# Cluster order of the last batch in a routed-attention and PReLU-MLP kernel: ranks found over three halves, one VectorE piece a slot, counts' product apart from the sums' product

## The chip, the cores and the metric

The kernel runs on one core of a Trainium2 chip. The metric is the device time of one execution in microseconds, median of three runs; less is better. Engines are named as in the profile: PE is TensorE, PEld its weight loads, DVE is VectorE, ACT is ScalarE, POOL is GpSimd, SP is the queue that issues most transfers.

## The reference

Inputs are q, k and v of 4 batches x 8 heads x 768 tokens x 64 features, 16 centroids a head, and the weights of a two-layer MLP of 512 -> 2048 -> 512 with a slope for each hidden unit.

```python
q_assign = np.argmax(np.einsum('bhsd,hcd->bhsc', q_n, c_n), axis=-1)
k_assign = np.argmax(np.einsum('bhsd,hcd->bhsc', k_n, c_n), axis=-1)
mask = q_assign[:, :, :, None] == k_assign[:, :, None, :]
scores = np.where(mask, scale * np.matmul(q, k.transpose(0, 1, 3, 2)), -1e9)
attn = softmax(scores)                      # over the keys of the same cluster
out = np.matmul(attn, v)                    # (B,H,S,D) -> x of (B*S, H*D)
h = x @ w_in
return (np.maximum(h, 0) + alpha * np.minimum(h, 0)) @ w_out
```

A query attends only to keys whose nearest centroid is its own. The MLP takes all heads of a token together.

## The kernel before

Heads are taken in pairs, four pairs a batch, sixteen in all (`n` = 0 to 15). A pair of batches 0 to 2 is worked off in two halves of 384 queries; the four pairs of the last batch (`n` = 12 to 15) are worked off whole. A half, or a whole pair of the last batch, is three *steps*, and from step 24 on its work is dealt out over 12 *slots* (two in the first step, five in each of the others). What a slot holds is written out by hand: `tick()` first runs the pieces that `later(slots, piece)` has put off to this slot, then one entry of `todo` (the masks and sums of the attention), then one entry of `sorting` (scatter work), then `feed` gives a share of MLP pieces of the *batch before*, so that PE always has dense work: a `hidden(f)` piece (four matmuls, L973, its copy out of PSUM on ACT, L979, and its slope on DVE, L965) or a `final` piece (four matmuls, L991). Each engine runs its own list in the order in which these Python calls emit instructions; the tile framework adds the waits.

The `todo` list of a half (L1173 to L1190) is: three masks, the five additions of the six exponentials (`add_up`, L770), `turn` (L789) and `rows_sums` (L795, writes `part`), two empty entries, and, in the half's last slot, `total` (L805): a small matmul that adds up the softmax denominators from `part`. Its result is written into `misc()`, a PSUM tile `mps` of a pool with **one** buffer (L89). Whatever matmul writes `mps` next waits until the reader of the last one is done. In the next half's beginning `invert` takes reciprocals of the total (L815), and `normalise` (L949) makes `xT`, the MLP's input.

The last batch is not masked over all keys. Its tokens are first put in the order of their clusters, so that a chunk of 128 queries need only see the neighbouring chunks of keys. That order is found ahead of time, in the middle of batches 1 and 2, at the steps `ORDERS = [30, 36, 54, 60]` (each the first step of a half), one for each pair:

- `load(n)` brings q and k, one step ahead;
- `order_features` (L535, two DVE transposes of 128x768) in steps t, t at slots 2 and 3;
- `order_sims` (L544), four matmuls with the centroids into `mps`, at t+1;
- `order_counts` (L549) one slot later: `argmax` (L376 to L393: transpose, maximum, compare, times rank, maximum), `only_first` (L396), a transpose to `mine` (L555) and a running count (`tensor_tensor_scan`, L557). These are eight DVE instructions in one go;
- `order_begins` (L564) at t+2, slot 2: two small matmuls of the counts, into `mps`;
- `order_ranks` (L572 to L592) one slot later: `begin` and `begins` are read from `mps` (L572, L573), then four more DVE instructions give each token its row, `off` (L581), and fill the `sorting` queue; `order_clusters` (L594) one slot later, three DVE instructions.

So everything from the transposes to the ranks falls in one half. After it the `sorting` entries load rows into two `stage` tiles (SP, L614) and scatter them into `scratch` in HBM (POOL, L625). Four steps before pair n begins (`u - 4`), `order_load` reads the sorted rows back (L636 to L654); `prep_clusters` (L425) makes the key clusters at `u - 3`, through `mps` and an ACT copy `every` (L429). After the attention of a pair in the last batch, `normalise_near` (L888) puts its result back in token order: `to_rows` (L911) turns it through `mps` in two parts, later by 4 and 6 slots, `put_back` (L919) scatters twelve pieces from slot 8 on, and `fetch_back` (L931) reads them at slot 14.

Of the kernel before, what the change touches and what calls it, by code (L numbers as in the profile page):

```python
# [23 lines left out]
def kernel(  # L24
# [70 lines left out]
    def later(slots, piece):  # L95
        due.setdefault(now[0] + slots, []).append(piece)
# [277 lines left out]
                             start=True, stop=True)  # L374
        later(1, lambda: prep_argmax(n, ps))

    def argmax(ps):
        simT = asg.tile([P, HS], FP32, name="simT")
        nc.vector.transpose(out=simT, in_=ps[:, 0:HS])
        sim = simT.rearrange("p (t c) -> p t c", c=NC)  # L380


        mx = asg.tile([P, 2 * NX], FP32, name="mx")
        nc.vector.tensor_reduce(out=mx, in_=sim, axis=AX.X, op=ALU.max)
        top = asg.tile([P, 2 * NX, NC], BF16, name="top")
        nc.vector.tensor_tensor(
            out=top, in0=sim, in1=mx[:, :, None].broadcast_to((P, 2 * NX, NC)),
            op=ALU.is_ge)
        nc.vector.tensor_tensor(
            out=top, in0=top, in1=rank[:, None, :].broadcast_to((P, 2 * NX, NC)),  # L390
            op=ALU.mult)
        first = asg.tile([P, 2 * NX], BF16, name="first")
        nc.vector.tensor_reduce(out=first, in_=top, axis=AX.X, op=ALU.max)  # L393
        return top, first

    def only_first(top, first):  # L396
        nc.vector.tensor_tensor(
            out=top, in0=top, in1=first[:, :, None].broadcast_to((P, 2 * NX, NC)),
            op=ALU.is_equal)

    def prep_argmax(n, ps):
        top, first = argmax(ps)
        firsts[n] = first
        if n >= NCH:
            return
        only_first(top, first)
        member = memp.tile([P, 2, HS], BF16, name="member")
        nc.vector.transpose(out=member[:, 0, :], in_=top.rearrange("p t c -> p (t c)"))

        def of_heads():  # L410
            for h in (1, 0):
                nc.scalar.activation(
                    out=member[HP:P, h, :], in_=member[HP:P, 0, :], func=AF.Identity,
                    scale=pick[HP:P, h:h + 1], bias=pick[HP:P, h + 2:h + 3])

        members[n] = member
        later(12 if n == 0 else 7, of_heads)
# [130 lines left out]

    def order_counts(n, ps):  # L549

        ordp = sorts["ordp"]
        top, first = argmax(ps)
        only_first(top, first)
        member = ordp.tile([P, HS], BF16, name="mine")
        nc.vector.transpose(out=member, in_=top.rearrange("p t c -> p (t c)"))  # L555
        count = asg.tile([P, HS], FP32, name="simT")
        nc.vector.tensor_tensor_scan(count, member, member, 0.0, ALU.add, ALU.max)  # L557
        us[n] = member, count

    def order_begins(n):  # L560
        member, count = us[n]
# [6 lines left out]
    def order_ranks(n, ps):  # L568
        member, count = us.pop(n)
        ordp, order = sorts["ordp"], sorts["order"]  # L570
        begin = ordp.tile([P, 2], FP32, name="begin")
        nc.vector.tensor_tensor(out=begin, in0=ps[:, 0:2], in1=sorts["shift"], op=ALU.add)  # L572
        nc.vector.tensor_copy(out=sorts["begins"][:, n - NO:n - NO + 1], in_=ps[:, 0:1])  # L573
        nc.vector.scalar_tensor_tensor(out=count, in0=count, scalar=begin[:, 1:2],
                                       in1=member, op0=ALU.add, op1=ALU.mult)
        by_token = ordp.tile([P, NX, 2, NC], FP32, name="by_token")
        nc.vector.transpose(out=by_token.rearrange("p x h c -> p (x h c)"), in_=count)
        rank = ordp.tile([P, NX, 2], FP32, name="rank")
        nc.vector.tensor_reduce(out=rank, in_=by_token, axis=AX.X, op=ALU.add)
        off = order.tile([P, NX, 2], I32, name="off")  # L580
        nc.vector.tensor_scalar(out=off, in0=rank, scalar1=0.0, scalar2=float(2 * S - 1),  # L581
                                op0=ALU.max, op1=ALU.min)
        ranks[n] = off
        whole = tc.dram_tile([2 * 2 * S, P], FP32, name=f"scratch{n}")
        scratch[n] = whole, dram_disjoint_views(whole, 2 * NX)
        for i in range(2 * PARTS + STAGES):
            if i >= STAGES:
                for x in range(NX // PARTS):
                    sorting.append(lambda i=i - STAGES, x=x: order_scatter(n, i, x))
            if i < 2 * PARTS:  # L590
                sorting.append(lambda i=i: order_stage(n, i))
        later(1, lambda: order_clusters(n, begin))  # L592

    def order_clusters(n, begin):  # L594
        ordp, order = sorts["ordp"], sorts["order"]
# [292 lines left out]
    def normalise_near(n):  # L888
        outT = inp.tile([P, 2, NJ, D], FP32, name="qk").rearrange("p h j d -> p (h j d)")
        for side in range(2):  # L890
            nc.vector.tensor_tensor(out=outT[:, side * HS:(side + 1) * HS],
                                    in0=pos.pop((n, side))[:, 0:HS],
                                    in1=rds.pop((n, side)), op=ALU.mult)
        whole = tc.dram_tile([2 * S, D], FP32, name=f"back{n}")
        to = dram_disjoint_views(whole, 2 * NJ)
        found = orders.pop(n)
        place = sorts["order"].tile([P, 2, NJ], I32, name="place")
        nc.vector.tensor_scalar(out=place, in0=found[:, :, :, 0], scalar1=0, scalar2=S - 1,
                                op0=ALU.max, op1=ALU.min)
        rows = sorts["byrow"].tile([P, NJ, P], FP32, name="rows")  # L900
        for i in range(2):
            later(4 + 2 * i, lambda i=i: to_rows(outT, rows, i))
        for i in range(2 * NJ):
            later(8 + i // 2, lambda i=i: put_back(to, place, rows, i))
        later(8 + NJ, lambda: fetch_back(n, whole))

    def to_rows(outT, rows, i):

        ps = misc()
        for j in range(HJ):  # L910
            nc.tensor.transpose(out=ps[:, j * P:(j + 1) * P],  # L911
                                in_=outT[:, (i * HJ + j) * P:(i * HJ + j + 1) * P],
                                identity=ident)
        later(1, lambda: nc.scalar.copy(  # L914
            rows[:, i * HJ:(i + 1) * HJ].rearrange("p j d -> p (j d)"), ps[:, 0:HS]))
# [109 lines left out]
    TOGETHER = 2 * UB  # L1025
    FREE = SLOTS * SB - 3

    ORDERS = [30, 36, 54, 60]
    prep_at, load_at = {}, {}
    for (n, half), u in start_of.items():  # L1030
        def at(step, slot, piece):
            prep_at.setdefault((step, slot), []).append(piece)
        if half is None:
            t = ORDERS[n - NO]
            load_at.setdefault(t - 1, []).append(lambda n=n: load(n))
            for i in range(2):
                at(t, FIRST + i, lambda n=n, i=i: order_features(n, i))
            at(t + 1, FIRST + 1, lambda n=n: order_sims(n))
            at(t + 2, FIRST, lambda n=n: order_begins(n))
            load_at.setdefault(u - 4, []).append(lambda n=n: order_load(n))  # L1040
            at(u - 3, FIRST, lambda n=n: prep_clusters(n))
            for i in range(2):
                at(u - 2, FIRST + i, lambda n=n, i=i: order_blocks(n, i))
                at(u - 1, FIRST + i, lambda n=n, i=i: order_queries(n, i))
            continue
        if half == 0:
            if n < NCH:
                if n > 1:
                    load_at.setdefault(max(u - 7, 0), []).append(lambda n=n: load(n))
                if n > 0:  # L1050
                    load_at.setdefault(max(u - 6, 0), []).append(lambda n=n: load_v(n))
            else:
                load_at.setdefault(u - 9, []).append(lambda n=n: load(n))
                load_at.setdefault(u - 7, []).append(lambda n=n: load_v(n))
            if n < NCH:
                for g in range(len(groups)):
                    at(u - 4, FIRST + g, lambda n=n, g=g: prep_features(n, g))
            else:
                for w in range(2):
                    at(u - 7, FIRST + w, lambda n=n, w=w: prep_blocks(n, w))  # L1060
            at(u - (3 if n < NCH else 5 if u - 6 < TOGETHER else 6), FIRST,
               lambda n=n: prep_sims(n))
            if n >= NCH:
                at(u - 4, FIRST, lambda n=n: prep_clusters(n))
        for h in range(2):
            at(u - 1, FIRST + h, lambda n=n, half=half, h=h: prep_queries(n, half, h))
# [363 lines left out]
```

## Time and profile before

| | |
|---|---|
| time, three runs | 1009.71, 1011.34, 1012.8 us; median 1011.34 us |
| profiled execution | span 1011.6 us, mean granted clock 0.989 |
| PE waits before `total` (L805) for `begins` (L573) | 12.0 us in 4 places, one at each order |
| scatters (L625) of the four pairs begin at | 298.57, 363.69, 549.42, 612.47 us |
| last batch's attention | about 699 to 807 us; from 840 us on only MLP is left |

The page gives for each engine its busy time. A busy engine isn't yet the bound: what counts is where PE stands still, for PE has the most work. The list of PE's waits names for each of its lines the instruction that ended the wait; the timeline of one engine shows what that instruction was queued behind. A matmul of fp32 operands shows as two records, so a `hidden` piece, four matmuls, is eight records. An ACT or DVE start in an answer may lie some hundredths of a microsecond before the end of its forerunner, since records overlap a little.

### The profile page before, as it was taken

To read this page: it belongs to the slowest core of one execution; us is meant where nothing else is said; L and a number is where in the kernel's file an instruction comes from. 1 tells how busy PE (TensorE), PEld (TensorE's weight loads), DVE (VectorE), ACT (ScalarE), POOL (GpSimd) and SP (SyncE) were. 2 spreads that over 40 slices of the span, in tenths; PEclk is the share of its full clock that TensorE was granted. 3 is DMA by queue.
4 is the path that set the end of the run, shared out by engine and by line. 5 is a ranking of instruction groups with operands and counts; after the bars stand their busy time and mean duration, and the time that the engine had idled before them with its cause. 6 is when DMAs were issued, how large, how long until landed. Compare 5 with 4: busy or idle time off the path is not lost.

```text
span 1011.6 us, 10921 instructions
## 1 busy us (share of the span) xinstructions
PE 974.3 (96%) x3955; PEld 484.7 (48%) x3955; DVE 655.0 (65%) x1209; ACT 259.6 (26%) x468; POOL 214.0 (21%) x249
## 2 busy tenths in 40 slices
PE   8889999999989999999999997999999999999997
PEld 5434444454444444545444444455554545455453
DVE  5887798598596785877859587678998723021010
ACT  5755443222221221312222122222132111110110
POOL 1423223000013534400002356300045440000000
PEclk9999999999999999999999998999999999999999
DMA  6533552050003422415000322600431120000000
GB/s 246 196 109 107 149 141 51 16 108 17 1 8 83 105 62 51 84 37 104 1 1 12 88 73 65 124 1 11 84 63 32 28 50 16 0 1 32 0 1 34
DMA packets 174286, 60.46 MB, mean 60 GB/s; under 512 B 161216, under 2 KB 164752, under 8 KB 174224
## 3 DMA queue, kind: packets, MB, share of 16 engines
q1 hardware_dynamic: 168768, 51.42, 21.5%
q0 software_dynamic: 4608, 7.87, 2.3%
q8 instruction: 33, 0.54, 0.2%
q10 hardware_dynamic: 848, 0.39, 0.2%
q14 instruction: 29, 0.24, 0.1%
HBM read 45.15 MB, written 14.16 MB: 59 GB/s over the span
## 4 chain that ended last, share of the span: by engine, by line
PE 84%; DVE 11%; ACT 2%; issue 2%; DMA 1%; ACTq 0%; DVEq 0%; POOL 0%; POOLq 0%
PE fps L991 32%; PE fps L973 27%; PE vps L849 8%; PE sps L719 7%; PE fps L719 3%; DVE acc L770 1%; DVE gT L965 1%; PE sps L728 1%; PE mps L371 1%; PE vps L885 1%; DVE acc L789 1%; DVE more L760 1%; DVE E L760 1%; DVE part L795 1%; ACT E L740 1%
## 5 line engine op out<-in xcount | busy, mean ns | idle before, releaser
L973 PE MATMUL fps<-xT,w_in_sb 128*128 128x384 f32 x1024 | 347.8, 494 | 0.8 <-issue 0.8
L991 PE MATMUL fps<-w_out_sb,gT 128*128 128x512 f32 x768 | 340.2, 598 | 3.4 <-issue 2.3
L973 PEld LDWEIGHTS fps<-xT,w_in_sb 128*128 128x128 f32 x1024 | 192.2, 192 | 140.9 <-issue 11.6
L991 PEld LDWEIGHTS fps<-w_out_sb,gT 128*128 128x128 f32 x768 | 144.2, 191 | 178.2 <-issue 168.1
L625 POOL DMA_INDIRECT scratch<-stage,off x96 | 104.8, 1092 | 291.8 <-DVE gT L965 125.8
L965 DVE SCALAR_TENSOR_TENSOR gT<-gT,alpha 128x384 f32<-128x384 f32 x128 | 80.3, 637 | 131.6 <-ACT gT L979 120.0
L979 ACT COPY gT<-fps 128x384 f32<-128x384 f32 x128 | 61.2, 478 | 364.6 <-PE fps L973 342.2
L719 PE MATMUL sps<-qkT 64*128 64x384 f32 (+1 forms) x512 | 96.5, 494 | 0.8 <-ACT E L740 0.8
L760 DVE SCALAR_TENSOR_TENSOR more<-aq,key,more 128x384 f32<-128x384 bf16 (+1 forms) x136 | 74.5, 603 | 24.2 <-ACT more L740 16.8
L740 ACT ACTIVATE E<-sps 128x768 f32<-128x768 f32 (+1 forms) x81 | 61.2, 801 | 78.0 <-PE sps L728 44.4
L919 POOL DMA_INDIRECT back<-rows,place x48 | 49.2, 1026 | 129.7 <-ACT rows L914 116.3
L999 DVE TENSOR_TENSOR y<-y,fps 128x512 f32<-128x512 f32 x30 | 20.6, 685 | 79.0 <-PE fps L991 79.0
L719 PEld LDWEIGHTS sps<-qkT 64*128 64x128 f32 x512 | 45.8, 186 | 45.1 <-issue 17.5
L849 PE MATMUL vps<-E,vt 128*64 128x384 f32 x356 | 66.6, 500 | 0.0
L760 DVE SCALAR_TENSOR_TENSOR E<-aq,key,E 128x384 f32<-128x384 bf16 (+1 forms) x104 | 57.1, 602 | 11.9 <-ACT E L740 6.7
L770 DVE TENSOR_TENSOR acc<-acc,E 128x768 f32<-128x768 f32 x47 | 44.9, 955 | 16.9 <-ACT E L740 15.4
L997 ACT COPY y<-fps 128x512 f32<-128x512 f32 x24 | 14.0, 585 | 135.1 <-PE fps L991 115.9
L740 ACT ACTIVATE more<-sps 128x768 f32<-128x768 f32 (+1 forms) x47 | 35.6, 796 | 40.2 <-PE sps L719 33.7
L849 PEld LDWEIGHTS vps<-E,vt 128*64 128x64 f32 x356 | 23.3, 138 | 32.6 <-issue 32.3
L849 PE MATMUL vps<-more,vt 128*64 128x384 f32 x220 | 38.8, 491 | 0.0
L269 POOL TENSOR_TENSOR w_in_sb<-w_in_sb,power 128x512 f32<-128x512 f32 x16 | 22.2, 1386 | 70.2 <-DVE w_in_sb L266 70.2
L719 PE MATMUL fps<-qkT 64*128 64x384 f32 x160 | 34.9, 508 | 0.0
(175 smaller groups left out, 731.4 us busy)
## 6 DMA issues: line engine op xcount, KB each, us to landing
raw<-in_moe_w_in_dram SPq DMA_DIRECT2D x16, 512.0 KB
raw<-in_moe_w_out_dram SPq DMA_DIRECT2D x16, 512.0 KB
out_dram<-y SPq DMA_DIRECT2D x24, 256.0 KB
vt<-in_v_dram SPq DMA_DIRECT2D x12, 384.0 KB
qk<-in_q_dram SPq DMA_DIRECT2D x48, 96.0 KB
qk<-in_k_dram SPq DMA_DIRECT2D x48, 96.0 KB
qk<-scratch SPq DMA_DIRECT2D x32, 96.0 KB
qk<-in_q_dram SPq DMA_DIRECT2D x4, 384.0 KB
```

What stands on the lines that cost most here:

```text
L269: nc.gpsimd.tensor_tensor(out=dst, in0=dst, in1=power[0].bitcast(FP32), op=ALU.mult)
L625: nc.gpsimd.indirect_dma_start(out=scratch[n][1][h * NX + xx], out_offset=bass.IndirectOffsetOnAxis(ap=ranks[n][:, xx, h:h + 1], axis=0), ...
L719: nc.tensor.matmul(out=bank(ps, h, m), lhsT=qkT[r:r + D, S + c * P:S + (c + 1) * P], rhs=qkT[r:r + D, tokens], start=True, stop=not early_ ...
L740: nc.scalar.activation(out=E[:, :, 0:m], in_=ps[:, :, 0:m], func=AF.Exp, scale=SCALE)
L760: nc.vector.scalar_tensor_tensor(out=e, in0=of, scalar=keys[n][:, NJ + c, h:h + 1], in1=e, op0=ALU.is_equal, op1=ALU.mult)
L770: nc.vector.tensor_tensor(out=acc, in0=acc if first is None else first[3], in1=E, op=ALU.add)
L849: nc.tensor.matmul(out=po[r:r + D, 0:HS], lhsT=vts[n][:, h, c, :], rhs=e[:, h, :], start=(c == 0), stop=(c == NJ - 1))
L919: nc.gpsimd.indirect_dma_start(out=to[i], out_offset=bass.IndirectOffsetOnAxis(ap=place[:, h, j:j + 1], axis=0), in_=rows[:, j, h * D:(h + ...
L965: nc.vector.scalar_tensor_tensor(out=gs[f], in0=gs[f], scalar=alpha[:, f:f + 1], in1=gs[f], op0=ALU.mult, op1=ALU.max)
L973: nc.tensor.matmul(out=ps[:, 0:HS], lhsT=w_in_sb[:, c, f * P:(f + 1) * P], rhs=xTs[b, half][:, c, :], start=(c == 0), stop=(c == NCH - 1))
L979: nc.scalar.copy(gs[f], ps[:, 0:HS])
L991: nc.tensor.matmul(out=ps[:, 0:DM], lhsT=gs[f][:, i * P:(i + 1) * P], rhs=w_out_sb[:, f, :], start=on and f == f0, stop=off and f == f0 + ...
```

## The change

The ordering of one pair is stretched over three halves, and its DVE instructions are dealt out one to a slot between the additions of the attention, in place of blocks of eight and six. Loads and transposes (`order_features`) come in the half before (t = `ORDERS` is three steps earlier, and they stand at t+2); the products with the centroids are at t+3, so in the same step of the same half as `ORDERS` before, one step earlier than the products were; the small matmuls of the counts (`order_begins`) move out of that half to the next one, t+7, away from the sums' product `total`. `order_ranks` is cut in two, the second part a slot later. `prep_clusters` moves from three to four steps before its pair. In the last batch `to_rows` comes 6 and 10 slots after `normalise_near` instead of 4 and 6, except for the very last pair, and each part's `put_back` follows two slots after it.

```diff
-    def argmax(ps):
+    def argmax(ps, exact):
...
+        pieces = [
+            lambda: nc.vector.transpose(out=simT, in_=ps[:, 0:HS]),
+            lambda: nc.vector.tensor_reduce(out=mx, in_=sim, axis=AX.X, op=ALU.max),
+            lambda: nc.vector.tensor_tensor(out=top, in0=sim, in1=wide(mx), op=ALU.is_ge),
...
     def prep_argmax(n, ps):
-        top, first = argmax(ps)
+        top, first, pieces = argmax(ps, exact=n < NCH)
+        for piece in pieces:
+            piece()
...
     def order_counts(n, ps):
-        top, first = argmax(ps)
-        only_first(top, first)
...
+        top, first, pieces = argmax(ps, exact=True)
...
+        for i, piece in enumerate(pieces):
+            later(i, piece) if i else piece()
...
+        later(1, lambda: order_rows(n, begin, count))
+
+    def order_rows(n, begin, count):
...
-        later(1, lambda: order_clusters(n, begin))
+        later(2, lambda: order_clusters(n, begin))
...
+        starts = (4, 6) if n == NP - 1 else (6, 10)
         for i in range(2):
-            later(4 + 2 * i, lambda i=i: to_rows(outT, rows, i))
-        for i in range(2 * NJ):
-            later(8 + i // 2, lambda i=i: put_back(to, place, rows, i))
-        later(8 + NJ, lambda: fetch_back(n, whole))
+            later(starts[i], lambda i=i: to_rows(outT, rows, i))
+            for x in range(NJ):
+                later(starts[i] + 2 + x // 2,
+                      lambda i=i, x=x: put_back(to, place, rows, i * NJ + x))
+        later(starts[1] + 2 + HJ, lambda: fetch_back(n, whole))
...
-    ORDERS = [30, 36, 54, 60]
+    ORDERS = [27, 33, 51, 57]
...
-            load_at.setdefault(t - 1, []).append(lambda n=n: load(n))
+            load_at.setdefault(t, []).append(lambda n=n: load(n))
             for i in range(2):
-                at(t, FIRST + i, lambda n=n, i=i: order_features(n, i))
-            at(t + 1, FIRST + 1, lambda n=n: order_sims(n))
-            at(t + 2, FIRST, lambda n=n: order_begins(n))
+                at(t + 2, 2 + 2 * i, lambda n=n, i=i: order_features(n, i))
+            at(t + 3, FIRST + 1, lambda n=n: order_sims(n))
+            at(t + 7, 2, lambda n=n: order_begins(n))
             load_at.setdefault(u - 4, []).append(lambda n=n: order_load(n))
-            at(u - 3, FIRST, lambda n=n: prep_clusters(n))
+            at(u - 4, FIRST, lambda n=n: prep_clusters(n))
```

More of the change, by code (lines that the diff above doesn't have):

```diff
@@ L375, in prep_sims, with wide @@
         later(1, lambda: prep_argmax(n, ps))
-    def argmax(ps):
+    def argmax(ps, exact):
         simT = asg.tile([P, HS], FP32, name="simT")
-        nc.vector.transpose(out=simT, in_=ps[:, 0:HS])
         sim = simT.rearrange("p (t c) -> p t c", c=NC)
         mx = asg.tile([P, 2 * NX], FP32, name="mx")
-        nc.vector.tensor_reduce(out=mx, in_=sim, axis=AX.X, op=ALU.max)
         top = asg.tile([P, 2 * NX, NC], BF16, name="top")
[L386 to L391, printed above, removed]
-        first = asg.tile([P, 2 * NX], BF16, name="first")
[L393 to L399, printed above, removed]
+        first = asg.tile([P, 2 * NX], BF16, name="first")
+        def wide(row):
+            return row[:, :, None].broadcast_to((P, 2 * NX, NC))
+        pieces = [
+            lambda: nc.vector.transpose(out=simT, in_=ps[:, 0:HS]),
+            lambda: nc.vector.tensor_reduce(out=mx, in_=sim, axis=AX.X, op=ALU.max),
+            lambda: nc.vector.tensor_tensor(out=top, in0=sim, in1=wide(mx), op=ALU.is_ge),
+            lambda: nc.vector.tensor_tensor(
+                out=top, in0=top, in1=rank[:, None, :].broadcast_to((P, 2 * NX, NC)),
+                op=ALU.mult),
+            lambda: nc.vector.tensor_reduce(out=first, in_=top, axis=AX.X, op=ALU.max)]
+        if exact:
+            pieces.append(lambda: nc.vector.tensor_tensor(
+                out=top, in0=top, in1=wide(first), op=ALU.is_equal))
+        return top, first, pieces
     def prep_argmax(n, ps):
-        top, first = argmax(ps)
+        top, first, pieces = argmax(ps, exact=n < NCH)
+        for piece in pieces:
+            piece()
         firsts[n] = first
@@ L549, in order_counts, with scan @@
     def order_counts(n, ps):
-        ordp = sorts["ordp"]
-        top, first = argmax(ps)
[L553 to L558, printed above, removed]
+        top, first, pieces = argmax(ps, exact=True)
+        member = sorts["ordp"].tile([P, HS], BF16, name="mine")
+        pieces.append(lambda: nc.vector.transpose(
+            out=member, in_=top.rearrange("p t c -> p (t c)")))
+        def scan():
+            count = asg.tile([P, HS], FP32, name="simT")
+            nc.vector.tensor_tensor_scan(count, member, member, 0.0, ALU.add, ALU.max)
+            us[n] = member, count
+        pieces.append(scan)
+        for i, piece in enumerate(pieces):
+            later(i, piece) if i else piece()
     def order_begins(n):
@@ L575, in order_ranks @@
                                        in1=member, op0=ALU.add, op1=ALU.mult)
+        later(1, lambda: order_rows(n, begin, count))
+    def order_rows(n, begin, count):
+        ordp, order = sorts["ordp"], sorts["order"]
         by_token = ordp.tile([P, NX, 2, NC], FP32, name="by_token")
```

## The prediction, made before the changed kernel was run

> **What bounds the kernel now.** First the page's busy shares, then PE's waits, then the timeline around the longest of them.
>
> ```profile
> PE 974.3 (96%) x3955; PEld 484.7 (48%) x3955; DVE 655.0 (65%) x1209; ACT 259.6 (26%) x468; POOL 214.0 (21%) x249
> ```
>
> PE works 974.3 of 1011.6 us, so at most 37.3 us can be won by keeping it fed. The list of PE's waits has one large line:
>
> ```profile
> PE mps L805 <- DVE begins L573: 12.0, 4, 4.8
> ```
>
> Four waits, one for each ordered pair, in front of the denominators' product. The timeline of all engines around the fourth (starts, duration, engine, line, tiles):
>
> ```profile
> 599.41 0.58 DVE L379 STREAM_TRANSPOSE simT<-mps 128x384 f32<-128x384 f32 x1 [1.61 <-PE mps L544]
> ...
> 603.40 0.96 DVE L557 TENSOR_TENSOR_SCAN simT<-mine 128x384 f32<-128x384 bf16 x1
> ...
> 606.12 1.14 DVE L965 SCALAR_TENSOR_TENSOR gT<-gT,alpha 128x384 f32<-128x384 f32 x2
> 607.17 0.97 DVE L789 STREAM_TRANSPOSE acc<-acc 128x768 f32<-128x768 f32 x1
> 608.18 0.95 DVE L795 TENSOR_REDUCE part<-acc 128x24 f32<-128x768 f32 x1
> 609.05 0.57 DVE L460 STREAM_TRANSPOSE aq<-every 128x384 bf16<-128x384 bf16 x1
> 609.54 0.12 DVE L572 TENSOR_TENSOR begin<-mps,shift 128x2 f32<-128x2 f32 x1
> 609.58 0.14 DVE L573 COPY begins<-mps 128x1 f32<-128x1 f32 x1
> ...
> 609.87 0.59 PE L805 MATMUL mps<-part,fold 128*128 128x24 f32 x2 [4.79 <-DVE begins L573]
> ...
> 610.29 5.11 PE L973 MATMUL fps<-xT,w_in_sb 128*128 128x384 f32 x8
> ```
>
> Two readings. PE's product waits for `begins`, which must leave the single `mps` buffer. But `part`, its own operand, ends only at 609.13, 0.6 us earlier: taking `begins` away alone would win 0.6 us. The queue in front of both is the argmax block, eight instructions from 599.41 to 604.36. And after the wait a hidden piece takes 5.11 us, where such a piece is 2.67 us elsewhere: PE ran at half clock.
>
> How crowded DVE is in the ordering halves and their next ones (columns: busy of PE, PEld, DVE, ACT, POOL, then clock, DMA share, GB/s):
>
> ```profile
> 276.00:299.00 23.00, 19.99 (x78) 11.10 (x78) 22.20 (x38) 4.73 (x10) 0.43 (x1) 1.00 0.00 1
> 299.00:334.00 35.00, 35.00 (x118) 16.24 (x120) 20.97 (x36) 6.15 (x11) 14.22 (x17) 1.00 0.31 74
> 590.00:615.00 25.00, 20.21 (x66) 11.07 (x64) 22.82 (x41) 4.03 (x8) 10.48 (x11) 0.86 0.15 41
> 615.00:647.00 32.00, 29.72 (x100) 13.55 (x98) 19.04 (x33) 6.79 (x12) 21.72 (x25) 0.95 0.62 123
> ```
>
> DVE is full at the orders (22.20 of 23) and has 13 to 14 us free in the halves after. Before the orders it idles too: 5.45 us at once before 582.37.
>
> [...] `part` sits behind the argmax it doesn't need, and 8 records of hidden work behind the product. [...] the second order's wait of 2.1 us also had a slow piece after it (4.31 us), the first of 3.0 and the third of 2.1 had none. [...] the page's q8 queue moved 0.54 MB in 33 packets, 16 KB each[...].
>
> **The change, part by part.** I work per order from PE's start of L805: the later of PE's arrival and the end of `part` plus 0.2 us of signalling (609.73 to 609.87 is 0.14).
>
> 1. Transposes (2 x 0.97 us) leave the crowded half. Only part is won: at 276.83 the first fills the gap before the masks, which wait for ACT's exponentials. Masks end 281.83 before; after, with six masks of 0.53 from 277.72 and the argmax's transpose of 0.58 put among them, 281.55: 0.3 us earlier. In the half before, the 1.94 us stand just ahead of `inv`, where DVE idles 2.45 us and more: nothing.
> 2. Products with the centroids one step earlier in PE's list: no work changes. At orders 2 to 4 DVE idled 1.61 us for them; they now come 8 to 12 hidden matmuls (over 5 us) earlier: 1.6 us of DVE won there, none at order 1.
> 3. Argmax dealt out: the same eight instructions. Seven remain ahead of `part`; the scan (0.98 us with its gap) falls behind it. The transpose's 0.58 us is counted in part 1. So `part` ends 0.3 + 0.6 + 1.0 = 1.85 us earlier at order 1, 3.45 at the others.
> 4. `order_begins` in the next half: L805 no longer waits for `aq`, `begin`, `begins`: 0.6 us. Its two matmuls (0.53 us) move along: the half sheds them, the next gains them.
> 5. With DVE earlier, its pair of slopes before `part` can wait for the fourth hidden piece. Orders 2 and 3 have six hidden pieces before the product, so DVE stalls about 1.6 us there, but PE arrives as late. Orders 1 and 4 have five: stall 0.2 and 0.
>
> L805 then starts, before -> after: order 1, 295.87 -> 293.7 (arrival 292.5, wait 1.2 left); order 2, 361.08 -> 358.7 (arrival sets it); order 3, 546.82 -> 544.5 (both); order 4, 609.87 -> 605.95 (wait 1.4 left). Each less 0.53 us given back: 1.65 + 1.85 + 1.8 + 3.4 = 8.7 us. The slow clock should go with the long waits: 4.31 - 2.67 at order 2, and 4.94 - 2.67 with 0.59 - 0.37 at order 4: 4.1 us. Sum won: 12.8 us.
>
> 6. Rows (3.6 us of DVE) in the next half: `part` there ended at 324.2, 386.6, 574.9 and 640.6, and PE's product began at 329.73, 394.25, 578.51 and 643.43. Slack is 5.5, 7.6, 3.6 and 2.8, plus 0.5 for the moved matmuls: nothing at three, 0.5 us at the last. The y additions (L999) are late by up to 1.7 us; their PSUM bank is needed 6.9 us later, one final group on. Nothing.
> 7. Scatters start some 20 us later (298.57 to about 322, 612.47 to about 635). The loads of the first sorted pair, issued at 626.92, go to about 645; their first reader on DVE (L661) is at 686.6. Hidden.
> 8. `prep_clusters` at `u - 4`: at three of the four pairs its four small matmuls now stand right ahead of a `total`, which waits for ACT's copy `every` (0.24 us) through the one buffer. Before shows that wait at 0.5 to 0.6 us: 3 x 0.55 = 1.65 added; the old places cost 0.42 + 0.47. Net +0.8.
> 9. `to_rows` spread: one wait of 0.95 us (761.70) goes, but in that half DVE, not PE, sets the end (`part` at 766.07), so I count nothing. Sorted rows return up to 2.2 us later to DVE, which may idle there: from 0 to 1 us a pair for two pairs; I take 0.
>
> Net: -12.8 + 0.5 + 0.8 = -11.5; 1011.34 - 11.5 = 999.8, I say **999.5 us**. Bounds: the slow pieces stay even after the short waits (+4.1) and part 9 costs 1: 1005; the waits at orders 1 and 4 vanish (-2.6): 997.
>
> **Rivals.** (B) [...] At 629.05 PE, ACT and DVE stand still together (PE 2.28 us, "issue"), while scatters and sorted loads share the DMA, and then four records take 3.19 us in place of 1.72. If this comes of the loads at 626.92, moving them removes 3.7 us: 996. [...] (C) Only the named wait goes: if DVE stays the last to end because interleaved pieces wait on each other or on the slopes, L805 gains just 0.6 us at each order, 2.4 in all, less 1.3: 1010.2, no change. For it: `part` is just 0.6 us ahead of `begins`. Against it: the 1.61 us and the scan leave DVE's queue in any case. (D) Slower: gains are lost to later scatters which [...]hold up outputs behind them in SP's queue; four stalls of 3.75 us against the 11.5 us give 1011.3 - 11.5 + 15 = 1014.8. For it: SP is one queue, and `stage` loads wait there for POOL. Against it: 686.6 - 645 leaves 40 us.
>
> **Chances.** 999.5 as worked out 0.70, B 0.17, C 0.06, D 0.07. The range 994.5 to 1005 takes the main case with its bounds and B, and leaves out C, D and the edges. Faster by over 0.3% (under 1008.3): 0.87; within: 0.06; slower: 0.07.
>
> **What would show it.** The wait of L805 for `begins` is gone; about 1 us for `part` remains at orders 1 and 4, none at 2 and 3; the hidden piece after each product takes 2.67 us. DVE's idle 1.61 us before `simT` is gone. Three waits of about half a microsecond for `every` appear before products after 640 us. Scatters start near 322 and 635 us. Wrong would be: slow pieces still there, DVE idle ahead of `part` at all orders, or new PE waits on y, `qkT` or DMA.

## The result, and the profile after

The changed kernel takes **1003.53 us** (median of four runs, 1003.52 to 1003.54), the kernel before 1010.72 us in the same comparison (1009.71 to 1012.8); ratio 0.9926, interval 0.9909 to 0.9943. The forecast was 999.5 us (994.5 to 1005): the direction is right and the time is in the range, but 4 us of the forecast 11.5 are missing. The account below shows that this is the sum of larger errors with opposite signs, so that the time falls in the range is in part luck: the orders won more than forecast, and two places lost what was not forecast.

The time of the kernel before moves with its granted clock: in the comparison of the last three experiments five of its eleven runs took 1010.4 to 1011.2 us at a mean clock of 0.987, five about 1008.7 at 0.990, and one 1004.65 at 0.995. The changed kernel has 0.994 or 0.995 in all its runs, so part of its 7.2 us is slow clock that most runs of the kernel before meet, but not all.

The page's first row, then the list of TensorE's waits of the changed kernel (total, times, longest; L817 is the sums' product, L805 before):

```profile
PE 968.5 (97%) x3955; PEld 482.1 (48%) x3955; DVE 650.4 (65%) x1209; ACT 259.6 (26%) x468; POOL 211.8 (21%) x249
```

```profile
PE mps L927 <- DVE inv L827: 4.2, 2, 2.7
PE mps L817 <- DVE part L807: 3.9, 3, 1.7
PE fps L989 <- DVE y L1015: 1.8, 1, 1.8
...
PE mps L817 <- ACT every L433: 1.6, 3, 0.6
...
PE mps L927 <- DVE qk L903: 1.2, 1, 1.2
...
PE fps L1007 <- ACT E L749: 1.0, 1, 1.0
```

The 12.0 us for `begins` are gone. In their place stand two waits of 1.07 us for `part` (first and fourth order), and a set of new ones: a row part (L927) waits for `inv`, a hidden piece (L989) for a y addition, and in the last batch the sums' product waits for `part` (1.75 us) and for `every`. The timeline around the fourth order, the place shown of before:

```profile
595.30 0.62 DVE L981 SCALAR_TENSOR_TENSOR gT<-gT,alpha 128x384 f32<-128x384 f32 x1 [0.78 <-ACT gT L995]
...
595.84 0.57 DVE L557 STREAM_TRANSPOSE mine<-top 128x384 bf16<-128x384 bf16 x1
596.33 0.93 DVE L801 STREAM_TRANSPOSE acc<-acc 128x768 f32<-128x768 f32 x1
...
597.30 0.95 DVE L807 TENSOR_REDUCE part<-acc 128x24 f32<-128x768 f32 x1
...
598.17 0.95 DVE L562 TENSOR_TENSOR_SCAN simT<-mine 128x384 f32<-128x384 bf16 x1
...
598.40 0.37 PE L817 MATMUL mps<-part,fold 128*128 128x24 f32 x2 [1.07 <-DVE part L807]
598.62 2.83 PE L989 MATMUL fps<-xT,w_in_sb 128*128 128x384 f32 x8
```

The scan now starts when `part` is done; the product waits 1.07 us instead of 4.79, and the piece after it takes 2.83 us instead of 5.11, so the slow clock is gone: over these pieces the mean granted clock is 1.00, and was 0.54 before. The sums' products, which occur once a half, give a ruler. Their starts, before and after:

| product | before | after | difference |
|---|---|---|---|
| first of the program | 113.89 | 114.45 | +0.56 |
| batch 1, second half of its first pair | 229.06 | 231.73 | +2.67 |
| first order | 295.87 | 296.06 | +0.19 |
| second order | 361.08 | 358.62 | -2.46 |
| third order | 546.82 | 539.79 | -7.03 |
| fourth order | 609.87 | 598.40 | -11.47 |
| next half | 643.43 | 625.68 | -17.75 |
| last of the last batch | 799.94 | 788.77 | -11.17 |
| end of the program | 1011.6 | 1001.4 | -10.2 |

The profiled execution of before took 1013.4 us, more than the median, so the ruler's end shows 10.2 us where the medians show 7.2. Within the ruler 2.1 us are lost between 204 and 229 us and 7.6 us after 643 us. The first loss, in the timeline of the changed kernel:

```profile
216.31 0.28 DVE L509 TENSOR_REDUCE cols<-simT 128x1 f32<-128x128 f32 x1
...
217.23 0.29 DVE L509 TENSOR_REDUCE cols<-simT 128x1 f32<-128x128 f32 x1 [0.64 <-POOL simT L508]
...
220.28 0.15 DVE L531 TENSOR_SCALAR shift<-shift 128x1 f32<-128x1 f32 x1
220.35 1.14 DVE L772 SCALAR_TENSOR_TENSOR E<-aq,key,E 128x384 f32<-128x384 bf16 x2
221.41 0.95 DVE L782 TENSOR_TENSOR acc<-more,more 128x768 f32<-128x768 f32 x1
222.28 0.68 DVE L1015 TENSOR_TENSOR y<-y,fps 128x512 f32<-128x512 f32 x1
...
223.01 2.20 PE L989 MATMUL fps<-xT,w_in_sb 128*128 128x384 f32 x6 [1.85 <-DVE y L1015]
```

These are the ordering's constants (`order_constants`), which the kernel makes in the step `u == ORDERS[0] - 2`. With 30 changed to 27 they moved from step 28 to step 25, without a line of the diff naming them. There they fill DVE for 4 us ahead of a y addition whose PSUM bank PE needs. In the kernel before they ran at 245 us and nobody waited.

The largest new wait of the last batch:

```profile
727.89 0.94 DVE L801 STREAM_TRANSPOSE acc<-acc 128x768 f32<-128x768 f32 x1
...
728.93 0.95 DVE L807 TENSOR_REDUCE part<-acc 128x24 f32<-128x768 f32 x1
...
729.80 0.30 DVE L827 RECIPROCAL inv<-mps 128x24 f32<-128x24 f32 x1
...
730.15 0.55 PE L927 MATMUL mps<-ident,qk 128*128 128x128 f32 x3 [2.68 <-DVE inv L827]
...
733.12 0.25 PE L429 MATMUL mps<-cluster,spread 128*128 128x24 bf16 x4
...
733.70 0.24 ACT L433 CAST every<-mps 128x96 bf16<-128x96 f32 x1
...
733.99 0.40 PE L817 MATMUL mps<-part,fold 128*128 128x24 f32 x2 [0.62 <-ACT every L433]
```

The second row part, now 10 slots after the normalisation, comes just after the first `total` of the next pair. The one `mps` buffer is free only when `inv` has read that total, and `inv` is queued on DVE behind the second side's `acc` and `part`. Next the clusters' matmul fills `mps`, and the second `total` waits for ACT's copy.

### The profile page after: what moved, and what is told of

Same layout as the page of the kernel before. It is cut to its first block, busy times and chain, and to the rows that moved or that the text cites. A ratio compares the mean times of both kernels' runs of the same rounds, so it can differ in the third digit from the quotient of the medians.

```text
span 1001.4 us, 10929 instructions
## 1 busy us (share of the span) xinstructions
PE 968.5 (97%) x3955; PEld 482.1 (48%) x3955; DVE 650.4 (65%) x1209; ACT 259.6 (26%) x468; POOL 211.8 (21%) x249
## 4 chain that ended last, share of the span: by engine, by line
PE 87%; DVE 8%; ACT 2%; issue 1%; DMA 1%; ACTq 0%; POOL 0%; DVEq 0%; POOLq 0%
PE fps L1007 31%; PE fps L989 31%; PE vps L861 8%; PE sps L731 7%; PE fps L731 3%; PE sps L740 1%; PE vps L897 1%; PE mps L371 1%; DVE gT L981 1%; DVE more L772 1%; PE mps L897 1%; DVE acc L801 1%; ACT E L752 1%; ACT member L416 1%; DMA aq<-member 1%
## 5 line engine op out<-in xcount | busy, mean ns | idle before, releaser
L989 PE MATMUL fps<-xT,w_in_sb 128*128 128x384 f32 x1024 | 342.9, 490 | 1.8 <-DVE y L1015 1.8
L989 PEld LDWEIGHTS fps<-xT,w_in_sb 128*128 128x128 f32 x1024 | 190.8, 190 | 140.5 <-issue 5.2
L637 POOL DMA_INDIRECT scratch<-stage,off x96 | 101.7, 1059 | 333.9 <-DMA stage<-in_v_dram 275.3
L782 DVE TENSOR_TENSOR acc<-acc,E 128x768 f32<-128x768 f32 x47 | 44.9, 955 | 16.7 <-ACT E L752 15.4
L269 POOL TENSOR_TENSOR w_out_sb<-w_out_sb,power 128x512 f32<-128x512 f32 x16 | 23.5, 1473 | 52.9 <-DVE w_out_sb L266 52.9
```

Of the source, the lines that this page charges most:

```text
L269: nc.gpsimd.tensor_tensor(out=dst, in0=dst, in1=power[0].bitcast(FP32), op=ALU.mult)
L637: nc.gpsimd.indirect_dma_start(out=scratch[n][1][h * NX + xx], out_offset=bass.IndirectOffsetOnAxis(ap=ranks[n][:, xx, h:h + 1], axis=0), ...
L782: nc.vector.tensor_tensor(out=acc, in0=acc if first is None else first[3], in1=E, op=ALU.add)
L989: nc.tensor.matmul(out=ps[:, 0:HS], lhsT=w_in_sb[:, c, f * P:(f + 1) * P], rhs=xTs[b, half][:, c, :], start=(c == 0), stop=(c == NCH - 1))
```

## The experiments

Theory: the orders won about what was forecast or more, and the two losses come of the moved constants and of the edits in the last batch. Rival: the waits in the last batch only change their place, because DVE sets the end there anyway (36.4 of the 40 us from 700 to 740 us in the profile of before), and the early loss too comes back at another place. All runs are given as ratios to the kernel before on the same chip; starts are from the profiled executions.

### The last batch undone in the changed kernel

```diff
-        starts = (4, 6) if n == NP - 1 else (6, 10)
...
+            later(4 + 2 * i, lambda i=i: to_rows(outT, rows, i))
...
-            at(u - 4, FIRST, lambda n=n: prep_clusters(n))
+            at(u - 3, FIRST, lambda n=n: prep_clusters(n))
```

> The changed kernel with its edits in the last batch undone: key clusters of the sorted pairs at u - 3 again, the two parts of the rows 4 and 6 slots after the normalisation, scatters from slot 8 on. Theory (the edits in the last batch cost what the ordering won: waits of the rows' products for inv 2.7 and 1.6 us and for qk 1.3, of the sums' product for part 1.75, three of about 0.5 for every, against 0.95, 0.42 and 0.47 us that come back): about 6 us faster than the changed kernel, 997.5 us (996 to 999.5). Rival (in these halves VectorE sets the end anyway, so PE's waits only change their place): within 1.5 us of the changed kernel, 1002 to 1004.

Measured: 994.28 us, ratio 0.9846 (0.9824 to 0.9869), more than was expected. Its ruler is 18.34 us ahead of before at the half after the fourth order and 18.96 us at the last product: nothing is lost in the last batch. The rival falls. The gain over the changed kernel, 9.2 us (9.0 in the profiles), is more than the 6 expected; two waits told of below, 1.0 and 1.25 us, are missing here as well.

### The last batch's edits alone, in the kernel before

The same lines, the other way round.

> The kernel before with only the edits in the last batch made (key clusters at u - 4, rows at 6 and 10 slots, scatters two slots after each). Theory that these edits cost about 6 us by themselves: 1017 us (1014 to 1019). Rival of the prediction, which counted them at 0.8 us with a bound of 2 more: 1011 to 1014. If the cost came only of an interplay with the moved ordering, no change: 1010 to 1012.

Measured: 1015.77 us, ratio 1.0056 (1.0035 to 1.0078), so these edits slow the kernel by themselves. From the half after the fourth order to the last product its ruler loses 5.5 us against before. Its list of PE's waits has the changed kernel's rows, with the old line numbers:

```profile
PE mps L805 <- DVE begins L573: 12.0, 4, 4.8
...
PE mps L913 <- DVE inv L815: 4.2, 2, 2.7
PE mps L805 <- ACT every L429: 2.2, 4, 0.6
PE mps L805 <- DVE part L795: 1.8, 1, 1.8
```

Two side results. Its profile has no standstill at 629 us, though its orders are those of before. And after the same wait of 3.00 us for `begins` at the first order a slow piece follows, 5.47 us at a granted clock of 0.50, where before had 2.83 at 1.00:

```profile
296.49 0.59 PE L805 MATMUL mps<-part,fold 128*128 128x24 f32 x2 [3.00 <-DVE begins L573]
296.91 5.47 PE L975 MATMUL fps<-xT,w_in_sb 128*128 128x384 f32 x8
```

### The constants back at step 28

```diff
-        if u == ORDERS[0] - 2:
+        if u == ORDERS[0] + 1:
```

> The changed kernel with the constants of the ordering made at step 28, where they were before, and not at step 25. Theory: their eleven VectorE instructions between 216.3 and 220.4 us put off the y addition for which PE's bank waits 1.85 us at 223.0; at step 28 they lie where VectorE has room: 1001.6 us, 1.9 faster than the changed kernel, and that wait is gone. Rival (the 2.65 us lost by step 30 are [...]a wait that comes back at another place): 1003 to 1004 us.

Measured: 999.71 us, ratio 0.9899 (0.9877 to 0.9921), 3.8 us below the changed kernel where 1.9 were expected. The y addition comes at once and PE goes on without a wait:

```profile
218.97 4.36 PE L989 MATMUL fps<-xT,w_in_sb 128*128 128x384 f32 x13
219.17 0.69 DVE L1015 TENSOR_TENSOR y<-y,fps 128x512 f32<-128x512 f32 x1 [0.30 <-PE fps L1007]
```

At the product after it this kernel is 1.57 us ahead of the changed one (230.16 against 231.73), though 0.55 us behind it until then. The rest of its 4.2 us in the profile are two waits that the changed kernel has and this one has not: 1.01 us for `E` at 638.80 and 1.25 us for `qk` at 799.37, where ACT and DVE stood still without a cause in the trace. These two are no work of the edit.

### Both repairs

> Both of the former: the changed kernel with the last batch as before and the constants at step 28. If both theories hold and the gains add: 995.5 us (994 to 998), below both kernels. If either cost was only moved: 1000 us and more.

Measured: **992.53 us**, ratio 0.9828 (0.9806 to 0.9851), the lowest ratio of all versions, below both kernels and below the expected range. What is left of PE's waits on `mps`:

```profile
PE mps L817 <- DVE part L807: 2.1, 2, 1.1
...
PE mps L925 <- ACT rows L928: 1.9, 2, 0.9
...
PE mps L925 <- ACT every L433: 1.0, 1, 1.0
...
PE mps L817 <- ACT every L433: 0.6, 1, 0.6
```

### The split of the products alone, in the kernel before

```diff
-            at(t + 2, FIRST, lambda n=n: order_begins(n))
+            at(t + 4, 2, lambda n=n: order_begins(n))
```

> The kernel before with one edit: the matmuls of the counts (order_begins) stand in the next half, two steps later at slot 2; everything else as before. The reasoning of the prediction's step 4 and rival C: the product L805 still has part to wait for, which ends 0.6 us before begins, so 4 x 0.6 = 2.4 us faster than before, a little more where a slow piece goes: 1008 us (1005.5 to 1009.5). Rival (the wait list is to be taken at its word: 12.0 us for begins, so the split alone carries the gain): 999 us and less.

Measured: ratio 0.9983 (0.9955 to 1.001), 1012.19 against 1013.34 us on a chip with more spread. No change can be told, and the rival (12 us) is out. The wait only changed its name (four of these five are at the orders, 11.3 us):

```profile
PE mps L805 <- DVE part L795: 11.7, 5, 4.6
```

### The split undone, in the version with both repairs

```diff
-            at(t + 7, 2, lambda n=n: order_begins(n))
+            at(t + 5, FIRST + 1, lambda n=n: order_begins(n))
```

> The version with both repairs (last batch as before, constants at step 28), and in it the matmuls of the counts put back into the half of the argmax, one slot ahead of the sums' product. Theory from its trace: at the first order begin would come after part, scan, the two transposes aq and a slope, so the product starts at about 296.5 in place of 294.5 us, 2.0 to 2.2 us later at each order; the next halves lose 0.3 us each: 992.5 + 7 = 999.5 us, up to 1003 if the slow pieces come back. Rival (the split is worth only the 0.6 us a pair that it took off before): 994 us.

Measured: 1013.66 us, ratio 0.9987 (0.9968 to 1.0007). The sums' products come 1.91, 2.42, 2.42 and 1.90 us later at the four orders, near what was expected. The slow pieces are back too (`296.44` below). The total is above the upper end. In the profiled execution, 1018.27 us and so nearly the slowest of 22, PE stands 8.53 us at 635.56 for a copy on ACT, which itself stands still; what holds up the runs around the median was not traced. The counts' products stand one slot ahead of `total` here, later than in the kernel before, and wait for the dealt-out scan.

```profile
294.98 0.58 PE L572 MATMUL mps<-simT,row 128*128 128x1 f32 x4 [1.93 <-DVE simT L562]
296.02 0.59 PE L817 MATMUL mps<-part,fold 128*128 128x24 f32 x2 [0.46 <-DVE begins L581]
296.44 5.47 PE L987 MATMUL fps<-xT,w_in_sb 128*128 128x384 f32 x8
```

### The argmax in one block again, in the version with both repairs

```diff
-            later(i, piece) if i else piece()
+            piece()
```

> The version with both repairs, with the eight instructions of argmax, transpose and scan in one block in the slot of the first, as they were. Only dealing them out is undone: the scan of 0.95 us is ahead of part again. Theory: part and the product come 0.9 to 1.0 us later at each of the four orders, as PE waits for part or arrives at most 0.2 us after it: 992.5 + 3.7 = 996.2 us (994.5 to 997.5). Rival (the block, once early, fills gaps in which VectorE waits for slopes, so that part comes no later): 992.5 us.

Measured: ratio 0.9846 (0.9812 to 0.9881), some 2 us above the version with both repairs, but the intervals overlap; the profiles tell more. They are put together here, as the time from the half before's product to that of the order:

| | order 1 | order 2 | order 3 | order 4 |
|---|---|---|---|---|
| before | 32.97 | 31.35 | 31.36 | 31.36 |
| split alone | 32.37 | 33.42 | 30.77 | 30.76 |
| earlier and dealt out, no split | 32.40 | 30.83 | 30.83 | 28.97 |
| earlier and split, in a block | 31.67 | 28.41 | 28.40 | 28.23 |
| all (changed kernel) | 30.49 | 28.41 | 28.41 | 27.06 |

(33.42 holds a standstill of PE of 2.38 us, which the trace puts to nothing.) The split alone wins 0.6 us at three orders, which is the distance from `part` to `begins`; at the second, with the standstill taken off, 0.3. Early products and dealing out without the split win 0.5 us at three orders and 2.4 at the fourth. Together they win 2.5 to 4.3, more than the two rows add up to. The reading is that while both heads of the queue were in one half, each hid the other; the earlier products by themselves, in a block and without the split, were not run. Dealing out alone is worth 1.2 us at the first and fourth order and nothing at the others, where PE's arrival sets the product. The expectation of 0.9 to 1.0 us at all four was wrong there.

### The clusters' edit alone

In the version with both repairs, `prep_clusters` at `u - 4`.

> The version with both repairs, but key clusters at u - 4 as in the changed kernel; the rows stay as before. Separates the two edits of the last batch. Theory (the rows' parts are what costs; the clusters cost the prediction's 0.8 us, three waits of 0.6 against 0.4 and 1.0 at the old places): 993.3 us (992.3 to 994.3). Rival (the clusters carry half of it or more): 996 to 998 us.

Measured: ratio 0.9853 (0.9815 to 0.9891). Its interval cannot separate the two expectations. In its profile it goes from 1.06 us ahead of the version with both repairs at the fourth order to 3.44 behind at the last product, 4.5 us; 2.5 of that are two standstills (three score records stretched at 632.94, and 1.24 us at 734.87) that no waiting instruction explains. What is left, some 2.0 us, is 0.9 at the first of its new places (the wait of 0.62 us and its own matmuls of 0.25) and 0.6 at two more, with nothing won back at the old one. The rows then have the rest of the 6.1 us that lie between the profiles of the version with the constants alone and of that with both repairs: about 4.1. This is a difference; the rows' edit was not run by itself.

### Three attempts on what is left

The second row part a slot later, in the version with the constants alone (`starts = (6, 11)`):

> The changed kernel with the constants at step 28, and the second part of the rows 11 slots after the normalisation in place of 10. Only at one pair does this put a final piece of 3.7 us ahead of that product on TensorE; there it waited 2.67 us for inv at 727.5 us. Theory (the product stood in TensorE's order ahead of work that was ready, because inv frees the one PSUM tile too late): that wait is gone and the time is 2.7 us below the version with the constants alone, a ratio to before of 0.987 where that version has 0.990. Rival (VectorE sets the end of this half, so the same time shows up at the next wait for part, 1.75 us at 750 us, which grows to over 4): 0.990.

Measured: ratio 0.9906 (0.9883 to 0.9928), no gain. I had read the order of one pair for another: the wait of 2.7 us at the earlier pair stayed, and a slow piece came after it (4.44 us). At the later pair there was no wait for `inv` to win. The changed kernel has one of 1.55 us there; the version with the constants alone has none, because PE arrives later by a slow piece:

```profile
753.02 3.68 PE L1007 MATMUL fps<-w_out_sb,gT 128*128 128x512 f32 x8
758.25 0.55 PE L927 MATMUL mps<-ident,qk 128*128 128x128 f32 x3 [1.55 <-DVE inv L827]
```

```profile
750.36 5.38 PE L1007 MATMUL fps<-w_out_sb,gT 128*128 128x512 f32 x8
755.59 0.55 PE L927 MATMUL mps<-ident,qk 128*128 128x128 f32 x3
```

The first two lines are of the changed kernel, the others of the version with the constants alone. With the later row part the product ahead of it, one half's sums, waited 2.13 us for `part` in place of 1.75, and new waits of 0.95 us for the copy `rows` stood before the clusters' matmul and a `total`. In these the time moves from wait to wait, as the rival has it, though `part` took 0.4 us of it and not the over 2 that it named.

The argmax two slots later, in the version with both repairs (`order_sims` at `t + 4`, slot 1):

> The version with both repairs, with the products with the centroids two slots later, so that three pieces of the argmax (comparison with the first, transpose, scan) in place of one come after part. Theory (the 1.07 us that TensorE still waits at the first and the fourth order is the DVE queue ahead of part, 0.55 and 0.57 us of it these two pieces): both waits go, 2.1 us, a ratio of 0.981 where the version with both repairs has 0.983. Rival (VectorE waits for the slopes of the last hidden pieces, so part comes no earlier): 0.983, waits still about 1 us.

Measured: ratio 0.9843 (0.9821 to 0.9865), no gain. Three pieces stand behind `part` now, and yet the product waits 1.07 and 1.42 us. DVE has no work there: its slope of a hidden piece waits for ACT's copy of that piece, as the rival said:

```profile
290.50 0.62 DVE L979 SCALAR_TENSOR_TENSOR gT<-gT,alpha 128x384 f32<-128x384 f32 x1 [1.60 <-ACT gT L993]
291.04 0.54 DVE L398 TENSOR_REDUCE first<-top 128x24 bf16<-128x384 bf16 x1
```

And with it the row parts further apart (`later(4 + 3 * i, ...)`):

> The former, and the second part of the rows in the last batch 7 slots after the normalisation instead of 6, so that a piece of dense work lies between the two parts. Theory (the waits of 0.95 us at two pairs for the copy rows are only TensorE at the one PSUM tile): both go, 1.9 us, a ratio of 0.979. Rival (the wait moves to total, which then waits for the copy rows): as the former.

Measured: ratio 0.9847 (0.9825 to 0.9869), no gain. The two waits of 0.95 us before a row part, at the second and the fourth pair, are gone. In their place two of the same length stand before `total`, at the first and the third pair, for the same copy, and one of 1.22 us for `part` at the second:

```profile
PE mps L817 <- ACT rows L928: 1.9, 2, 0.9
```

A second buffer for `mps` would be the direct test of the coupling. It was not run.

## Why the prediction was right or wrong

**Right: the mechanism at the orders.** The wait for `begins` went, about 1 us for `part` stayed at orders 1 and 4 (forecast 1.2 and 1.4, measured 1.07 each), none at 2 and 3. The step from `begins` to `part`, 0.6 us, was measured by itself as 0.6 at three orders. VectorE's idle 1.61 us before `simT` is gone. The reading that `part` was held up by the argmax queued ahead of it on VectorE agrees with the runs: with the argmax again in one block ahead of it, `part` and the product come 1.2 us later at orders 1 and 4. What counts is the queue ahead of `part`, not the last name in the wait.

**Mis-sized: the gain there.** The products gained 2.48, 2.94, 2.95 and 4.30 us, 12.7 in all, where the working had 10.8. The slow clock gave the 4.1 us that were forecast. In the timeline the pieces of 4.47 and 5.11 us (mean granted clock 0.62 and 0.55) became 2.83 (1.00), and the product of 0.59 became 0.37; the 4.31, 4.94 and 2.67 of the prediction are the same pieces counted without the overlap with their forerunner. Of the 2.1 us to be given back in the next halves (part 4) only some 0.65 can be seen: 0.29 after the first order, 0.37 after the third once a wait of 0.51 us of before is taken out, and next to nothing after the other two. The halves won 16.7 us, with the 3.75 us standstill of before left aside, instead of 12.8. Part 5 had the stalls of DVE for a slope too small, 0.2 and 0 us at orders 1 and 4 and 1.6 at the others, where 0.77, 0.78 and 1.96 were measured; the argmax run two slots later shows that this stall, and not the queue, keeps up the wait of 1.07 us at the first order. Why PE arrives half a microsecond earlier than worked out at orders 2 and 3 was not pursued.

**Missed: the constants.** No part of the working asks what else hangs on `ORDERS`. A new wait on y, which the prediction names as a sign of being wrong, is what came of it. It cost 1.85 us of wait, 2.1 at the next product; undoing it gave 2.65 us in the profile up to the last product, 1.1 of it by the E wait.

**Wrong: part 9, the rows.** It said "nothing" for PE and 0 to 1 us a pair for the sorted rows' way back, since DVE and not PE sets the end of that half. What it did not trace is who frees `mps` at the new slot. The rows cost about 4.1 us by the difference above. In the changed kernel PE waits 2.68 and 1.55 us for `inv`; in the version with the constants alone the second wait is gone, and the piece ahead of it is 1.70 us longer (5.38 us in place of 3.68). That DVE sets the end was said of one half, and there it held: the wait for `part` grew from 0.38 to 1.75 us. The waits for `inv` arise in the halves into which the second row parts move, and the working did not price those.

**Mis-sized: part 8, the clusters.** The waits after 640 us are there, three in the changed kernel: 0.62 us at 654.38, which the profile books as issue, 0.33 at 680.11 and 0.62 at 733.99 (forecast 0.55 each). One of the three in the list of waits above is another, 0.62 us at 231.73, which the kernel before has too. The forecast credit of 0.9 us for the old places was not won back, and the matmuls came along: 2.0 us in place of 0.8.

**Right: parts 6 and 7.** PE's products in the next halves wait for nothing (`part` at 624.21 there, the product at 625.68). Scatters start at 325.88 and 620.75 us (forecast 322 and 635 on the time of before, which by the second is some 12 to 18 us behind), and no reader of the sorted rows waits for them.

**The rivals.** B's event happened, the standstill at 629 us is gone, but its cause fell: the version with the last batch's edits alone has the orders where they were and the loads at 629.40 us, and its profile has no standstill there either. Other versions show such standstills elsewhere (2.38, 1.24, 8.53 us). That instruction fetches cause them was not shown: in the trace of before the instruction queues have no packet of 16 KB from 611 to 648 us, and one of 8 KB at 627.6. What the standstills are stays open. C (0.6 us an order) is what the split does alone. D found nothing.

In sum: forecast -11.5; the orders 3.9 better, part 6's 0.5 not needed, the start and the constants 2.7 worse, the last batch 6.8 worse than its 0.8 (with the 2.3 us of the two waits for `E` and `qk`, which are no part of the edits). That is -6.4 us for the profile without the standstill, where the medians say -7.2.

## What to carry to other kernels

When an edit shifts a schedule's anchor, list every statement that is placed relative to it, and price each at its new place. For each instruction that is moved through a single-buffered tile, name the reader that frees the tile at the new place, and what that reader is queued behind on its own engine. A wait named after one instruction may hide a second head of the queue just behind it; taking only one away wins the distance between the two (here 0.6 us at three orders).

## What was unexpected of the hardware

The slow clock does not follow from a wait's length alone. The first order's 3.0 us wait was followed by a piece of 2.83 us in the kernel before (mean granted clock 1.00) and by one of 5.47 us (0.50) in the version with the last batch's edits alone, whose schedule differs only after 640 us. Of the waits of 2.1 us at the second and third order, the second had the slow piece in the kernel before (4.47 us at 0.62, the third 2.83 at 1.00), and the third in that version (4.35 us, the second 2.83). A wait of 1.75 us had one in the version with the constants alone (5.38 us in place of 3.68) and none in the changed kernel (3.68 us at 1.00). Such a wait so cost up to 2.6 us more than its own length (5.47 less 2.83), but not every time. Why like waits end differently was not shown.
